# Three VectorE steps and one GpSimd step become two of each and a product: the exponentials that ScalarE does not take

## The chip, the cores and the metric

The kernel runs on one core of a Trainium2 chip. The metric is the device time of one execution in microseconds (us); three runs of the kernel before are given, and one further execution was recorded by the hardware profiler. The engines are TensorE (PE in the profile), VectorE (DVE), ScalarE (ACT), GpSimd (POOL) and SyncE (SP), which issues most transfers.

## The reference, cut to what matters

The kernel computes `g * a + (1 - g) * b` for one sequence of 2048 rows of 1024 values in bf16. `g` is a sigmoid of a row sum, `a` a diagonal state-space layer (a complex recurrence over 2048 steps between two large products), and `b` attention over all rows (no mask):

```
q, k, v = split(x @ wqkv)          # 32 heads of 32
scores  = q @ k.T * 32 ** -0.5
p       = softmax(scores)
b       = (p @ v) @ wo
```

The softmax needs 32 x 2048 x 2048 exponentials, 134 million. They are the largest single piece of elementwise work, and the change is in how a small part of them is computed.

## The kernel before, in words

**Attention.** The 32 heads are taken in 8 groups of 4 heads, the queries of a group in 8 blocks of 256, the keys of a block in 8 bursts of 256. That makes 512 bursts, numbered p = 0 to 511; `pg` is the number within a group, 0 to 63. In a burst TensorE computes the scores of 4 heads x 256 queries x 256 keys (line L1624, eight matmuls into two of three score buffers in PSUM), ScalarE takes their exponential in two instructions of 128x1024 (L1643), and TensorE later multiplies the result with the values (L1709). After the eight bursts of a block VectorE divides by the row sums (L1722, L1723) and a transposing transfer puts the result into place (L1729).

**The exponentials that VectorE takes.** In some bursts ScalarE's second instruction covers only 768 of the 1024 columns (L1640). The other 256 go to VectorE: L1633 reads them from PSUM, scales them and stores a fixed-point number in the tile `xi`, whose upper 16 bits are the integer part and lower 16 bits the fraction of a power of two. ScalarE's instruction of that burst waits for L1633, because both read the same score buffer. Two such bursts make a pair of 128x512, which `x_ops` finishes: a cubic polynomial of the fraction `lo`, put together with the integer part `hi` so that the bits of a bf16 number come out. Before the change these are three steps of VectorE in f32 (L1667, L1668, L1664, all `scalar_tensor_tensor`, which is an operation with a scalar and two tensors) and one of GpSimd (L1665), which rounds to the 16 bits. Line L1688 is the matmul that uses the result.

`X_PLAN` lists the pairs. Each entry is a burst number divisible by 4; within a block of eight bursts, a block with two entries takes bursts 0, 2 and 4, 6, and a block with one entry takes bursts 0 and 4 (`X_AT`).

**Dense work between the bursts.** TensorE fills each burst with four large matmuls of other work, through one PSUM bank: projections of the next group (`d_qk` L1426, `d_v` L1445), the state-space layer's input product (`d_u`, L1457) and output product (`d_c`, L1504), and at the end the output product with `wo` (`d_out`, L1535). When such a chain ends, VectorE empties the bank (L1433, L1451, L1461, L1517, L1547), and the next chain waits for that. VectorE also does the recurrence itself, called items: four products, two scans (L1362) and sums on SBUF tiles (L1353). GpSimd copies the last state of a scan (L1365) and carries it on (L1396).

**What sets the order.** Every engine's program is written out in a fixed order by `build`, which keeps a model of VectorE's clock (`dve_t`): for each burst it puts as many waiting VectorE steps into the queue as fit by their listed costs, the steps of `x_ops` preferred where no chain ends in the burst. A step of `x_ops` has a cost in the first place of its tuple; nothing at run time reorders a queue. Semaphores between the engines follow from the tiles that each step reads and writes.

**Weights.** The projection weights lie in the tile `wb`: those for K and V in two buffers by the parity of the group, those for Q in one. `ld_w` loads 256 KB; K and V of group g+2 are loaded at pg = 25 of group g, Q of group g+1 at pg = 28. The rows of `wo` are later loaded into parts of `wb` and of the tile `cT`. `C_LOADS` is the burst from which the transposed loads of the C matrices start (L1081). All these go through SP's queue, as do the stores and loads of the items' inputs (L1462, L1474).

Of the kernel before, what the change touches and what calls it, by code (L numbers as in the profile page):

```python
# [922 lines left out]
GROUPS = 8  # L923
# [9 lines left out]
C_LOADS = 28  # L933

X_AT = ((0, 2), (4, 6), (0, 4))
X_PLAN = (64, 72, 80, 88, 92, 96, 100, 104, 108, 112, 116, 120, 124, 128, 132, 136, 144, 152, 160, 168, 172, 176, 180, 184, 188, 192, 200, 208, 216, 224, 228, 232, 236, 240, 244, 248, 252, 256, 260, 264, 272, 280, 288, 296, 304, 312, 316, 320, 324, 328, 332, 336, 344, 352, 356, 360, 364, 368, 372, 376, 380, 384, 388, 392, 396, 400, 404, 408, 412, 416, 420, 424, 428, 432, 436, 440, 444, 448, 452, 456, 460, 464, 468, 472, 476, 480, 484, 488, 492, 496, 500, 504)
X_COLS = 256
F_TS, F_ST = 1.32, 1.24
I_MM = 0.61
X_LAST = 0.735  # L940
# [4 lines left out]
E3, E2, E1, E0 = 0.0780245226404788, 0.2260671649, 0.6958335355, 0.9999252185627155  # L945
X_K = 128.0 * E3 / 65536.0 ** 3
# [12 lines left out]
class FastPath:  # L959

    def __init__(self, nc, S, es, d, flag):
        self.nc, self.S, self.d, self.flag = nc, S, d, flag
        E = es.enter_context
        T = lambda name, shape, dt: E(nc.sbuf_tensor("f_" + name, shape, dt))
# [8 lines left out]
        wb = T("wb", [128, 8192], BF)  # L973
        self.wq = wb[:, 0:1024].rearrange("p (a n) -> p a n", a=8)
        self.wkv = wb[:, 1024:5120].rearrange("p (s q a n) -> p s q a n", s=2, q=2, a=8)
        self.bT = wb[:, 5120:8192].rearrange("p (s a n) -> p s a n", s=3, a=8)

        row = lambda o, n: wb[:, o:o + 1024 * n].rearrange("p (a n) -> p a n", a=n)
        self.wo3 = [row(1024, 2), row(5120, 3), row(3072, 1), self.cT[0][:, 0:1, :], self.cT[0][:, 1:2, :]]
        self.wo = [(self.wo3[0][:, a, :], "wo0") for a in range(2)] + [(self.wo3[4][:, 0, :], "wo4")] + [(self.wo3[1][:, a, :], "wo1") for a in range(3)]  # L980
        self.wo += [(self.wo3[3][:, 0, :], "wo3"), (self.wo3[2][:, 0, :], "wo2")]
# [3 lines left out]
        hp = T("hp", [128, 2, 8, 512], BF)  # L985
        self.hp = hp
        self.hpx = wb[:, 5120:8192].rearrange("p (k n) -> p k n", k=6)
# [5 lines left out]
        self.xp = T("xp", [128, 2 * X_COLS], BF)  # L993
        self.ut = T("ut", [128, 2, 512], F32)
# [70 lines left out]
    def w_of(self, g, part):  # L1065
        return (self.wkv[:, g % 2, part - 1], ("w", g % 2, part)) if part else (self.wq, ("w", 0, 0))
# [586 lines left out]
    def x_ops(self, b):  # L1653

        xi, xq, xp = self.xi[:, b % 2], self.xq, self.xp
        lo = xi.bitcast(mybir.dt.uint16)[:, 0::2]
        hi = xi.bitcast(mybir.dt.int16)[:, 1::2]
        bits = xp.bitcast(mybir.dt.int16)[:]
        w = 65536.0
        i2, p2 = [("xi", b % 2, 0), ("xi", b % 2, 1)], [("xp", 0), ("xp", 1)]  # L1660

        def last():
            assert self.x_out == len(self.x_done)
            self.dve(lambda e: e.scalar_tensor_tensor(xq[:], hi, 128.0 / X_K, xq[:], ALU.mult, ALU.add), i2 + ["xq"], ["xq"], "x_q")  # L1664
            self.pool(lambda e: e.tensor_scalar(bits, xq[:], X_K, 128.0 * (E0 + 126.0), ALU.mult, ALU.add), ["xq"], p2, "x_p")  # L1665
            self.x_done.add(b)
        return [(0.73, 0.0, lambda: self.dve(lambda e: e.scalar_tensor_tensor(xq[:], lo, E2 / E3 * w, lo, ALU.add, ALU.mult), i2, ["xq"], "x_q")),  # L1667
                (0.73, 0.0, lambda: self.dve(lambda e: e.scalar_tensor_tensor(xq[:], xq[:], E1 / E3 * w * w, lo, ALU.add, ALU.mult), ["xq"] + i2, ["xq"], "x_q")),  # L1668
                (X_LAST, 0.0, last)]

# [63 lines left out]
    def build(self):  # L1734
# [10 lines left out]
        for part in (1, 2):  # L1745
            self.ld_w(1, part)
# [12 lines left out]
        for g in range(1, GROUPS):  # L1759
            for c in range(4):  # L1760
                proj[g][8 + c].after = max(16 * c, 32)
        proj[0] = [self.d_qk(0, 0, 2), self.d_qk(0, 0, 3)]
        us, cs = [], []
# [15 lines left out]
        outs, k = [], 0  # L1779
# [3 lines left out]
        cur = None  # L1783
        first = FIRST
        wo1 = wo6 = last = False
# [4 lines left out]
        for p in range(first, NBURST):  # L1790
            g, pg = divmod(p, 64)
# [48 lines left out]
            if p == 386:  # L1840
                self.dma(lambda e: e.dma_start(self.wo3[0], wsv[:, 0:2, :]), [], ["wo0"] + [("w", 0, q) for q in (1, 2)], "ld_wo")
            if not cs and cur is None and not wo1 and self.c_left[3] == 0:
                wo1 = True
                self.dma(lambda e: e.dma_start(self.wo3[1], wsv[:, 3:6, :]), [], ["wo1"] + [("bT", r) for r in range(3)] + [("hp", 8, k) for k in range(6)], "ld_wo")
            if g >= 6 and not wo6 and not cs and self.c_left[3] == 0:
                wo6 = True
                self.dma(lambda e: e.dma_start(self.wo3[3], wsv[:, 6:7, :]), [], ["wo3", ("cT", 0, 0), ("cTf", 0, 0, 0), ("cTf", 0, 0, 1)], "ld_wo")
                self.dma(lambda e: e.dma_start(self.wo3[4], wsv[:, 2:3, :]), [], ["wo4", ("cT", 0, 1), ("cTf", 0, 1, 0), ("cTf", 0, 1, 1)], "ld_wo")
            if g >= 6 and not last and not proj[7] and not us and not cs and cur is None and not self.bg:

                last = True
                xs = [("xr", r) for r in range(16)]
                assert wo1 and wo6
                self.dma(lambda e: e.dma_start(self.wo3[2], wsv[:, 7:8, :]), [], ["wo2"] + [("w", 1, q) for q in (1, 2)] + xs, "ld_wo")
# [101 lines left out]
    def tail(self):  # L1956
# [41 lines left out]
        for r in range(2):  # L1998
            for cb in range(2):
                bank = 2 + r + 2 * cb  # L2000
                w = dict(acc=[("tb", bank)]) if cb == 0 else dict(writes=[("tb", bank)] + ([("S", 2)] if r == 0 else []), **({} if r == 0 else dict(acc=[("S", 2)])))
                S.op("pe", lambda e, r=r, cb=cb, bank=bank: e.matmul(ps[:, bank, :], OT[:, 7, 1792 + 128 * r:1920 + 128 * r], wo[7][0][:, 512 * cb:512 * (cb + 1)],
                                                                    start=(cb == 1), stop=True), reads=[("OT", 7, 7, r), "wo2"], name="tail", **w)
# [132 lines left out]
```

## Time and profile before

| | |
|---|---|
| median of 3 runs | 927.41 us (926.35 to 927.49) |
| profiled execution, its own time | 928.11 us |
| its span, first to last instruction | 926.3 us |
| granted TensorE clock, mean | 0.996 |
| ScalarE busy | 907.3 us, 98% |
| TensorE busy | 902.5 us, 97% |
| VectorE busy | 758.4 us, 82% |
| GpSimd busy | 86.8 us, 9% |
| pairs taken by VectorE | 92 |

The page gives each engine's busy time, the span in 40 slices with the busy share in tenths, the chain of work that ended last, and the costliest groups of instructions: line, engine, operation, output<-inputs, shapes, count, then busy time and mean duration, then the idle time before them and who ended it. The timeline gives the start, the length and the engine of single instructions, merged where they follow each other; idle time before an instruction stands in square brackets with its releaser. A mean of ScalarE's instructions is longer than their spacing, because one begins before the last has ended; spacing is read from starts.

### The profile page before, as it was taken

The page shows a single profiled execution, that of the slowest core. Times are in us where ns is not written, and L with a number is a line of the kernel's source. Part 1 is how long each engine was busy: PE and PEld are TensorE (multiplying, and loading weights), DVE is VectorE, ACT ScalarE, POOL GpSimd, SP SyncE. Part 2 cuts the span into 40 slices and gives each one's busy share as a digit, 9 for nine tenths or more (in the row PEclk, how much of TensorE's full clock was granted, in tenths as well). Part 3 has the DMA queues.
Part 4 walks back from the last instruction along what each step waited for, and adds up shares of the span by engine and source line. Part 5 has one row for each costly group of instructions (what it writes and reads, how often), then busy time and mean ns, then how long its engine had stood idle before and what let it go on. Part 6 is the DMA issues. An engine that isn't in the chain of part 4 may idle for free.

```text
span 926.3 us, 33979 instructions
## 1 busy us (share of the span) xinstructions
PE 902.5 (97%) x15316; PEld 503.9 (54%) x15316; DVE 758.4 (82%) x1310; ACT 907.3 (98%) x1034; POOL 86.8 (9%) x156
## 2 busy tenths in 40 slices
PE   8899999999999999999999999999999999999996
PEld 4554754557555565546655565555655655445553
DVE  2788989998989999989989999899988655776665
ACT  6999999999999999999999999999999999999996
POOL 2000000111000101011111020000010010001010
PEclk9999999999999999999999999999999999999998
DMA  9569747750457101272012511413001112424312
GB/s 195 87 116 184 93 84 138 144 116 5 81 113 152 50 20 49 67 147 53 19 51 65 126 45 31 104 63 103 20 15 43 31 51 77 156 83 128 114 62 75
DMA packets 170934, 77.69 MB, mean 84 GB/s; under 512 B 147232, under 2 KB 155424, under 8 KB 170784
## 3 DMA queue, kind: packets, MB, share of 16 engines
q1 hardware_dynamic: 168624, 74.94, 36.3%
q8 instruction: 121, 1.98, 0.9%
q10 hardware_dynamic: 2160, 0.53, 0.3%
q14 instruction: 29, 0.24, 0.1%
HBM read 25.18 MB, written 20.97 MB: 50 GB/s over the span
## 4 chain that ended last, share of the span: by engine, by line
PE 52%; ACT 40%; DVE 4%; DMA 2%; SPq 1%; issue 1%; POOL 0%; DVEq 0%; ACTq 0%
ACT f_pt L1643 32%; PE f_ps L1709 14%; PE f_ps L1624 10%; PE f_ps L1426 9%; PE f_ps L1504 7%; PE f_ps L1457 6%; ACT f_pt L1640 5%; PE f_ps L1445 5%; SPq L1062 1%; ACT f_cT L1643 1%; PE f_ps L1688 1%; DMA f_xT<-in_A_x_dram 1%; ACT f_Et L1643 1%; DMA f_wb<-in_A_B_im_dram 1%; DMA f_ub<-u_scratch 0%
## 5 line engine op out<-in xcount | busy, mean ns | idle before, releaser
L1643 ACT ACTIVATE f_pt<-f_ps 128x1024 bf16<-128x1024 f32 x760 | 728.8, 1090 | 1.5 <-PE f_ps L1624 1.3
L1709 PEld LDWEIGHTS f_ps<-f_V,f_pt 128*128 128x128 bf16 x7184 | 222.2, 96 | 95.3 <-issue 68.7
L1709 PE MATMUL f_ps<-f_V,f_pt 128*128 128x33 bf16 x7184 | 258.0, 178 | 0.0
L1624 PE MATMUL f_ps<-f_Q,f_K 32*128 32x256 bf16 x4096 | 203.3, 273 | 10.8 <-ACT f_pt L1643 3.3
L1640 ACT ACTIVATE f_pt<-f_ps 128x768 bf16<-128x768 f32 x184 | 165.3, 898 | 0.7 <-PE f_ps L1624 0.6
L1624 PEld LDWEIGHTS f_ps<-f_Q,f_K 32*128 32x128 bf16 x4096 | 60.7, 92 | 148.0 <-ACT f_pt L1643 120.6
L1457 PE MATMUL f_ps<-f_xT,f_wb 128*128 128x512 bf16 x512 | 131.5, 379 | 1.6 <-DMA f_wb<-in_A_B_im_dram 0.7
L1665 POOL TENSOR_SCALAR f_xp<-f_xq 128x512 int16<-128x512 f32 x92 | 67.3, 732 | 646.0 <-DVE f_xq L1664 471.3
L1426 PE MATMUL f_ps<-f_xT,f_wb 128*128 128x512 bf16 x464 | 119.3, 379 | 0.1
L1633 DVE TENSOR_SCALAR f_xi<-f_ps 128x256 int32<-128x256 f32 x184 | 77.4, 421 | 17.6 <-PE f_ps L1624 13.3
L1362 DVE TENSOR_TENSOR_SCAN f_ht<-f_pf,f_init,f_ut 128x512 bf16<-128x512 f32 x64 | 81.3, 1279 | 0.0
L1504 PE MATMUL f_ps<-f_cT,f_hp 128*128 128x512 bf16 x272 | 74.5, 379 | 0.1
L1667 DVE SCALAR_TENSOR_TENSOR f_xq<-f_xi 128x512 f32<-128x512 uint16 x92 | 63.7, 692 | 3.2
L1668 DVE SCALAR_TENSOR_TENSOR f_xq<-f_xq,f_xi 128x512 f32<-128x512 f32 x92 | 63.6, 692 | 3.1
L1664 DVE SCALAR_TENSOR_TENSOR f_xq<-f_xi,f_xq 128x512 f32<-128x512 int16 x92 | 63.5, 690 | 2.6
L1457 PEld LDWEIGHTS f_ps<-f_xT,f_wb 128*128 128x128 bf16 x512 | 40.1, 96 | 40.5 <-issue 8.6
L1535 PE MATMUL f_ps<-f_wb,f_OT 128*128 128x512 bf16 x188 | 61.2, 381 | 0.4 <-DVE f_Et L1547 0.4
L1445 PE MATMUL f_ps<-f_wb,f_xT 128*128 128x128 bf16 x896 | 59.3, 219 | 0.0
L1426 PEld LDWEIGHTS f_ps<-f_xT,f_wb 128*128 128x128 bf16 x464 | 36.1, 96 | 35.6 <-issue 7.6
L1461 DVE CAST f_ub<-f_ps 128x512 bf16<-128x512 f32 x64 | 44.1, 688 | 10.4 <-PE f_ps L1457 9.7
L1445 PEld LDWEIGHTS f_ps<-f_wb,f_xT 128*128 128x128 bf16 x896 | 50.4, 97 | 3.8 <-issue 3.8
L1722 DVE RECIPROCAL f_rc<-f_ps 128x8 f32<-128x8 f32 x63 | 13.1, 207 | 47.6 <-PE f_ps L1688 43.5
(149 smaller groups left out, 822.5 us busy)
## 6 DMA issues: line engine op xcount, KB each, us to landing
u_scratch<-f_ub SPq DMA_DIRECT2D x64, 128.0 KB, 2.1
f_ub<-u_scratch SPq DMA_DIRECT2D x32, 256.0 KB, 3.0
ag_scratch<-f_Ag SPq DMA_DIRECT2D x32, 256.0 KB, 2.0
f_hp<-ag_scratch SPq DMA_DIRECT2D x32, 256.0 KB, 3.0
f_wb<-in_B_wqkv_dram SPq DMA_DIRECT2D x21, 256.0 KB, 4.1
out_dram<-f_xT SPq DMA_DIRECT2D x16, 256.0 KB, 2.2
f_OT<-f_On SPq DMA_TRANSPOSE x63, 2.3
f_wb<-in_B_wo_dram SPq DMA_DIRECT2D x1, 768.0 KB
```

Source lines behind the costliest of these rows:

```text
L1362: ops.append((1.24, lambda ri=ri: dve(lambda e: e.tensor_tensor_scan(ht[:, ri, :], rr, ut[:, ri, :], self.init[:, ri, j:j + 1], ALU.mult, ...
L1426: mms.append((1, lambda e, f, l, a=a, w=w: e.matmul(ps[:, bank, :], w[:, a, :], xT[:, a, 512 * ch:512 * (ch + 1)], start=f, stop=l), [tok] ...
L1445: m = e.matmul(ps[:, bank, 128 * q:128 * (q + 1)], xT[:, a, 128 * kt:128 * (kt + 1)], w[:, a, :], start=(a == 0), stop=(a == 7))
L1457: mms.append((1, lambda e, f, l, a=a: e.matmul(ps[:, 7, :], bT[:, (2 * n + ri) % 3, a, :], xT[:, a, 512 * ch:512 * (ch + 1)], start=f, sto ...
L1504: mms.append((1, lambda e, f, l, j=j, ri=ri, h=h: e.matmul(ps[:, 7, :], h[:, cols], cT[ri][:, j, 512 * cb:512 * (cb + 1)], start=f, stop=l ...
L1624: m = e.matmul(ps[:, 2 * sl[h // 2] + h % 2, 256 * kl:256 * (kl + 1)], K[32 * h:32 * h + 32, g % 2, 128 * kt:128 * (kt + 1)], Q[32 * h:32 ...
L1633: first = self.dve(lambda e: e.tensor_scalar(self.xi[:, b % 2, X_COLS * n:X_COLS * (n + 1)], ps[:, 2 * s + 1, 512 - X_COLS:512], X_A, X_LO ...
L1640: self.S.op("act", lambda e: e.activation(flat(self.tile[p]), flat(ps[:, 2 * s:2 * s + 2, :]), ACT.Exp, scale=SCALE), reads=[("S", s)], wr ...
L1643: self.act(lambda e: e.activation(self.tile[p], ps[:, 2 * s:2 * s + 2, :], ACT.Exp, scale=SCALE), [("S", s)], [("pt", p)], "exp")
L1665: self.pool(lambda e: e.tensor_scalar(bits, xq[:], X_K, 128.0 * (E0 + 126.0), ALU.mult, ALU.add), ["xq"], p2, "x_p")
L1667: return [(0.73, 0.0, lambda: self.dve(lambda e: e.scalar_tensor_tensor(xq[:], lo, E2 / E3 * w, lo, ALU.add, ALU.mult), i2, ["xq"], "x_q") ...
L1709: m = e.matmul(ps[:, 6, o:o + 33], self.tile[p][:, h2, 256 * kl + 128 * qt:256 * kl + 128 * (qt + 1)], V[:, g % 2, 2 * i + kl, h, :], star ...
```

## The change: what it does

The cubic has one real root, -X_R, so it factors into (lo + X_R) times a quadratic. GpSimd now makes the linear factor first (`x_l`, 16-bit integers to f32, written to the new tile `xl`) and then the power of two (`x_e`, from `hi`, written as bf16 bits to the new tile `xe`). VectorE makes the quadratic's first part (`x_q`, as before), then the product of quadratic and linear factor (`x_m`, f32 in, bf16 out, new tile `xm`), and last the product of `xm` and `xe` in bf16 (`x_p`). The order of emission is: `x_l` on GpSimd, `x_q` on VectorE, `x_e` on GpSimd, `x_m`, `x_p`. The planned cost of the last step goes from 0.735 to 0.36.

Eight entries are added to `X_PLAN` (84, 204, 268, 276, 284, 292, 300, 308), so 100 pairs; in each case a block with one entry becomes a block with two. To make room for the new tiles `wb` shrinks from 8192 to 6144 columns: the weights of K and V have one buffer instead of two. Their loads move to pg = 0 of the group before (for group 1, V's at the start and K's at burst 17), Q's load to pg = 38, and the projections of K start no earlier than pg = 4, those of Q no earlier than pg = 42. The C loads start at burst 32 instead of 28. The rows of `wo` have new places, and seven of the eight are loaded together when the last output product of the state-space layer is done.

```diff
-C_LOADS = 28
+C_LOADS = 32
+W_AT = (38, 0, 17)
...
-X_LAST = 0.735
+X_LAST = 0.36
...
-X_K = 128.0 * E3 / 65536.0 ** 3
+X_R = 1.8383391859372556
+X_B, X_C = E2 / E3 - X_R, E0 / (E3 * X_R)
...
-        wb = T("wb", [128, 8192], BF)
+        wb = T("wb", [128, 6144], BF)
+        self.wqkv = [wb[:, 1024 * k:1024 * (k + 1)].rearrange("p (a n) -> p a n", a=8) for k in range(3)]
...
+        self.xl = T("xl", [128, 2 * X_COLS], F32)
+        self.xm = T("xm", [128, 2 * X_COLS], BF)
+        self.xe = T("xe", [128, 2 * X_COLS], BF)
...
     def w_of(self, g, part):
-        return (self.wkv[:, g % 2, part - 1], ("w", g % 2, part)) if part else (self.wq, ("w", 0, 0))
+        return self.wqkv[part], ("w", 0, part)
...
-        bits = xp.bitcast(mybir.dt.int16)[:]
+        bits = self.xe.bitcast(mybir.dt.int16)[:]
...
+        def start():
+            self.pool(lambda e: e.tensor_scalar(self.xl[:], lo, E3 / w ** 3, E3 * X_R / w ** 2, ALU.mult, ALU.add), i2, ["xl"], "x_l")
+            self.dve(lambda e: e.scalar_tensor_tensor(xq[:], lo, X_B * w, lo, ALU.add, ALU.mult), i2, ["xq"], "x_q")
+            self.pool(lambda e: e.tensor_scalar(bits, hi, 128.0, 128.0 * 127.0, ALU.mult, ALU.add), i2, ["xe"], "x_e")
+
         def last():
             assert self.x_out == len(self.x_done)
-            self.dve(lambda e: e.scalar_tensor_tensor(xq[:], hi, 128.0 / X_K, xq[:], ALU.mult, ALU.add), i2 + ["xq"], ["xq"], "x_q")
-            self.pool(lambda e: e.tensor_scalar(bits, xq[:], X_K, 128.0 * (E0 + 126.0), ALU.mult, ALU.add), ["xq"], p2, "x_p")
+            self.dve(lambda e: e.tensor_tensor(xp[:], self.xm[:], self.xe[:], ALU.mult), ["xm", "xe"], p2, "x_p")
             self.x_done.add(b)
-        return [(0.73, 0.0, lambda: self.dve(lambda e: e.scalar_tensor_tensor(xq[:], lo, E2 / E3 * w, lo, ALU.add, ALU.mult), i2, ["xq"], "x_q")),
-                (0.73, 0.0, lambda: self.dve(lambda e: e.scalar_tensor_tensor(xq[:], xq[:], E1 / E3 * w * w, lo, ALU.add, ALU.mult), ["xq"] + i2, ["xq"], "x_q")),
+        return [(0.73, 0.0, start),
+                (0.73, 0.0, lambda: self.dve(lambda e: e.scalar_tensor_tensor(self.xm[:], xq[:], X_C * w * w, self.xl[:], ALU.add, ALU.mult), ["xq", "xl"], ["xm"], "x_m")),
                 (X_LAST, 0.0, last)]
...
-        for part in (1, 2):
-            self.ld_w(1, part)
+        self.ld_w(1, 2)
...
-            if pg == 25 and g + 2 < GROUPS:
-                assert g or not (proj[0] or cur and cur.tag == "proj")
-                for part in (1, 2):
-                    self.ld_w(g + 2, part)
-            if pg == 28 and g + 1 < GROUPS:
-                assert not (cur and cur.tag == "proj")
+            if pg == W_AT[1 if g else 2] and g + 1 < GROUPS:
+                self.ld_w(g + 1, 1)
+                if g:
+                    self.ld_w(g + 1, 2)
+            if pg == W_AT[0] and g + 1 < GROUPS:
+                assert not proj[0]
                 self.ld_w(g + 1, 0)
```

More of the change, by code (lines that the diff above doesn't have):

```diff
@@ L1760, in build @@
             for c in range(4):
-                proj[g][8 + c].after = max(16 * c, 32)
+                proj[g][c].after = W_AT[1] + 4
+                proj[g][8 + c].after = max(16 * c, W_AT[0] + 4)
         proj[0] = [self.d_qk(0, 0, 2), self.d_qk(0, 0, 3)]
@@ L1784, in build @@
         first = FIRST
-        wo1 = wo6 = last = False
+        wo1 = last = False
         nal = nc = 0
@@ L1838, in build @@
+            if pg == W_AT[0] and g + 1 < GROUPS:
+                assert not proj[0]
                 self.ld_w(g + 1, 0)
             wsv = self.d["B_wo"].rearrange("(a p) n -> p a n", p=128)
-            if p == 386:
-                self.dma(lambda e: e.dma_start(self.wo3[0], wsv[:, 0:2, :]), [], ["wo0"] + [("w", 0, q) for q in (1, 2)], "ld_wo")
-            if not cs and cur is None and not wo1 and self.c_left[3] == 0:
+            if not wo1 and not cs and cur is None and self.c_left[3] == 0:
@@ L1843, in build @@
                 wo1 = True
[L1844 to L1848, printed above, removed]
+                for a in range(7):
+                    j = a if a < 3 else a - 3
+                    x = [("cT", 0, j), ("cTf", 0, j, 0), ("cTf", 0, j, 1)]
+                    if a in (3, 4, 5):
+                        x = [("bT", a - 3)] + [("hp", 8, k) for k in (2 * a - 6, 2 * a - 5)]
+                    self.dma(lambda e, a=a: e.dma_start(self.wo[a][0], wsv[:, a, :]), [], ["wo%d" % a] + x, "ld_wo")
@@ L1849, in build @@
             if g >= 6 and not last and not proj[7] and not us and not cs and cur is None and not self.bg:
                 last = True
-                xs = [("xr", r) for r in range(16)]
-                assert wo1 and wo6
-                self.dma(lambda e: e.dma_start(self.wo3[2], wsv[:, 7:8, :]), [], ["wo2"] + [("w", 1, q) for q in (1, 2)] + xs, "ld_wo")
+                assert wo1
+                self.dma(lambda e: e.dma_start(self.wo[7][0], wsv[:, 7, :]), [], ["wo7", ("cT", 0, 4), ("cTf", 0, 4, 0), ("cTf", 0, 4, 1)], "ld_wo")
```

16 lines of the change are left out of this document (7 added, 9 removed).

## Prediction

> **What bounds the kernel now.** I read the page's first two parts, the groups, and then the same busy times by stage.
>
> ```profile
> span 926.3 us, 33979 instructions
> PE 902.5 (97%) x15316; PEld 503.9 (54%) x15316; DVE 758.4 (82%) x1310; ACT 907.3 (98%) x1034; POOL 86.8 (9%) x156
> ...
> DVE  2788989998989999989989999899988655776665
> ACT  6999999999999999999999999999999999999996
> ```
>
> ```profile
> 140.00:700.00 560.00, 556.11 (x9501) 311.60 (x9501) 506.19 (x816) 559.22 (x638) 62.20 (x100) 1.00 0.33 74
> 700.00:926.30 226.30, 215.59 (x3617) 116.30 (x3615) 148.93 (x304) 218.18 (x253) 18.53 (x31) 0.98 0.27 82
> ...
> 500.00:540.00 40.00, 39.58 (x656) 21.01 (x649) 37.51 (x60) 40.00 (x46) 5.27 (x6) 1.00 0.44 106
> ```
>
> The columns after the stretch's length are TensorE, its weight loads, VectorE, ScalarE and GpSimd. ScalarE is busy in 559.2 of the 560 us between 140 and 700: its exponentials bound that stage. VectorE is at 506.2 of 560, 90%, and its fullest row of 40 us is 37.5, 94%, with ScalarE still at 40.0. After 700 it has room: 148.9 of 226.3. So columns moved off ScalarE shorten the kernel as long as VectorE keeps up, and in the long middle stage it has about 50 us in hand, part of it waits that it can't use.
>
> **What a pair is worth to ScalarE.** Its own timeline, where the plan passes from one pair per eight bursts to two:
>
> ```profile
> 547.50 0.98 ACT L1640 ACTIVATE f_pt<-f_ps 128x768 bf16<-128x768 f32 x1
> ...
> 554.62 0.98 ACT L1640 ACTIVATE f_pt<-f_ps 128x768 bf16<-128x768 f32 x1
> ...
> 572.37 0.93 ACT L1640 ACTIVATE f_pt<-f_ps 128x768 bf16<-128x768 f32 x1
> 573.11 2.93 ACT L1643 ACTIVATE f_pt<-f_ps 128x1024 bf16<-128x1024 f32 x3
> 575.84 0.91 ACT L1640 ACTIVATE f_pt<-f_ps 128x768 bf16<-128x768 f32 x1
> 576.55 2.95 ACT L1643 ACTIVATE f_pt<-f_ps 128x1024 bf16<-128x1024 f32 x3
> 579.27 0.93 ACT L1640 ACTIVATE f_pt<-f_ps 128x768 bf16<-128x768 f32 x1
> ```
>
> With one pair, four bursts take 554.62 - 547.50 = 7.12 us, eight 14.24. With two pairs two bursts take 3.47 and 3.43, eight 13.80. The eight blocks that get a second pair give 8 x 0.44 = 3.5 us, if nothing else stops ScalarE.
>
> **The pair on VectorE, before.**
>
> ```profile
> 571.51 0.41 DVE L1633 TENSOR_SCALAR f_xi<-f_ps 128x256 int32<-128x256 f32 x1
> 571.96 0.69 DVE L1667 SCALAR_TENSOR_TENSOR f_xq<-f_xi 128x512 f32<-128x512 uint16 x1
> 572.68 0.69 DVE L1668 SCALAR_TENSOR_TENSOR f_xq<-f_xq,f_xi 128x512 f32<-128x512 f32 x1
> 573.41 0.69 DVE L1664 SCALAR_TENSOR_TENSOR f_xq<-f_xi,f_xq 128x512 f32<-128x512 int16 x1
> 574.07 0.69 DVE L1433 CAST f_Q<-f_ps 128x512 bf16<-128x512 f32 x1
> ...
> 574.19 0.62 POOL L1665 TENSOR_SCALAR f_xp<-f_xq 128x512 int16<-128x512 f32 x1 [7.64 <-DVE f_xq L1664]
> ```
>
> L1633's second half of the pair ends at 571.92; the three steps follow back to back and end at 574.10, 2.18 us later. The dense bank's cast starts at once behind them. GpSimd's step, 0.62 us, starts 0.09 after the third step and runs beside the cast, which reads PSUM.
>
> **The pair after, if the two engines didn't disturb each other.** The first step is the old one (0.69), `x_m` has its shape (0.69), and `x_p`, a product of 512 bf16 columns, is like the 0.42 of this row:
>
> ```profile
> L1353 DVE TENSOR_TENSOR f_hp<-f_ut,f_tq 128x512 bf16<-128x512 bf16 x17 | 7.1, 417 | 0.0
> ```
>
> GpSimd's `x_l` would start 0.09 after L1633 and end at 0.71, so `x_m` starts about 0.77, after the 0.73 of `x_q`; `x_e` is done by 1.3, before `x_m` at 1.5. The chain ends about 1.9 after L1633: 0.28 less than before.
>
> **But they share something.** These rows, VectorE's and GpSimd's, are what the forecast turns on:
>
> ```profile
> 267.97 1.28 DVE L1320 SCALAR_TENSOR_TENSOR f_cT<-f_cT,f_pf,f_OT 128x1024 bf16<-128x1024 bf16 x1
> ...
> 268.13 1.59 POOL L1665 TENSOR_SCALAR f_xp<-f_xq 128x512 int16<-128x512 f32 x1 [10.90 <-DVE f_xq L1664]
> ...
> 550.62 1.28 DVE L1362 TENSOR_TENSOR_SCAN f_ht<-f_pf,f_init,f_ut 128x512 bf16<-128x512 f32 x1
> 551.93 0.91 DVE L1353 TENSOR_TENSOR f_tq<-f_ht,f_Et 128x1024 bf16<-128x1024 bf16 x1
> ...
> 550.79 1.52 POOL L1665 TENSOR_SCALAR f_xp<-f_xq 128x512 int16<-128x512 f32 x1 [12.13 <-DVE f_xq L1664]
> ...
> L1353 DVE TENSOR_TENSOR f_ut<-f_ht,f_Et 128x1024 bf16<-128x1024 bf16 x32 | 21.9, 685 | 0.0
> ```
>
> The same GpSimd step takes 0.62 beside a cast from PSUM and 1.52 to 1.59 beside a VectorE operation that reads two SBUF tensors. It ends a fixed time after that operation: 268.13 + 1.59 = 269.72, 0.47 after 269.25; 552.31, 0.41 after 551.90. It is held until VectorE's operation is over. The other way round, the product that starts at 551.93 under a running GpSimd step takes 0.91 instead of 0.685 and ends 0.53 after that step. One of the two waits for the other.
>
> Before the change GpSimd's step mostly falls beside a cast. Now both of its steps are released by L1633, at the moment when VectorE starts `x_q`, and all of `x_q`, `x_m`, `x_p` read two SBUF tensors. VectorE is first: in the rows above it starts 0.04 after L1633, GpSimd 0.09 after its releaser. So, counted from the end of L1633:
> - `x_q` 0.04 to 0.73; `x_l` is held and ends 0.41 to 0.48 later, at 1.14 to 1.21. `x_m` waits for it.
> - `x_e` is next in GpSimd's queue, already released, and runs another 0.57 to 0.62, to about 1.75; `x_m`, started beside it, is held and ends 0.53 later, at 2.28.
> - `x_p` 0.42 and a gap of 0.03: 2.73.
> If `x_m` gets in ahead of `x_e`, it ends at 1.93, `x_e` at 2.4, `x_p` at 2.86. So the chain is 0.55 (to 0.68) us longer than before, not 0.28 shorter; the plan, which reserves 0.73 + 0.73 + 0.36 = 1.82, fills the difference with other steps and is 0.9 short per pair. I take +0.55, since it follows from the row with a product behind GpSimd; the ends for the range are -0.28 and +0.68.
>
> The Trainium skill states the rule behind these rows ("SBUF — State Buffer", section "Who interferes with whom"): a VectorE instruction with two SBUF inputs contends with a GpSimd instruction that reads SBUF, and the second to issue fully blocks until the first is done. The trace agrees that one blocks, but of GpSimd's 0.62 us only 0.41 to 0.48 come after the release, so a part of it is not blocked. By full blocking, 0.73 + 0.62 + 0.62 + 0.69 + 0.45, the chain would be 3.1 us, and the sum below would come out 70 x 0.38 / 0.98 = 27 us higher. The rows have durations for it, so they are used.
>
> **What that costs.** How many pairs fall into each stage:
>
> ```profile
> 140.00:700.00 560.00, 42.72 (x62) 1.00 0.33 74
> 700.00:926.30 226.30, 20.77 (x30) 0.98 0.27 82
> ```
>
> Middle stage: 506.2 + 62 x 0.55 (34) + 8 new pairs x (2 x 0.42 for L1633 + 2.73) (29) = 569, less some 4 us by which the old GpSimd step held products (an estimate: the 64 of the row below are each 0.027 longer than 0.685, 1.7 us, and the other products are held likewise), so 565 us of VectorE's time in a stage that is 560 long and that ScalarE alone would shorten to 556.5.
>
> ```profile
> L1353 DVE TENSOR_TENSOR f_ut<-f_ht,f_tq 128x512 f32<-128x512 bf16 x64 | 43.4, 712 | 0.7
> ...
> DVE f_rc L1722 <- PE f_ps L1688: 43.5, 50, 1.8
> ```
>
> VectorE becomes the bound, and its queue is in order: L1633 (on which ScalarE waits) and the casts of the single dense bank (on which TensorE waits, and behind TensorE's wait the next scores) stand behind the chain. At 100% busy the stage is 565 long (+5), at the 94% of the fullest row 601 (+41). VectorE's largest idle time is its wait for a block's last matmul, 43.5 us in all in 50 waits; that shrinks when VectorE is the late one, so I take 98%: 576, +16.
>
> Late stage: 30 pairs, VectorE at 66%. What stands behind the chain there:
>
> ```profile
> 867.49 0.75 DVE L1547 SCALAR_TENSOR_TENSOR f_xT<-f_ps,f_gcol,f_hp 128x512 bf16<-128x512 f32 x1
> ...
> 868.47 0.59 PE L1535 MATMUL f_ps<-f_wb,f_OT 128*128 128x512 bf16 x2
> 869.49 0.12 PEld L1624 LDWEIGHTS f_ps<-f_Q,f_K 32*128 32x128 bf16 x8 [0.49 <-ACT f_pt L1643]
> ```
>
> The bank is read out by 868.24, the next chain starts 0.23 later, and TensorE then waits 0.49 for ScalarE. A delay of 0.55 becomes one of 0.3 on TensorE, which that wait covers: 0, at most 30 x 0.2 = 6. I take +1.
>
> **Transfers.** The opening has one stall that the moves touch:
>
> ```profile
> 68.14 1.28 SPq L1071 DMA_DIRECT2D f_wb<-in_B_wqkv_dram  x1
> 69.53 0.67 SPq L1474 DMA_DIRECT2D f_ub<-u_scratch  x1
> ...
> 73.34 0.69 DVE L1353 TENSOR_TENSOR f_ht<-f_ub,f_Et 128x1024 bf16<-128x1024 bf16 x1 [2.39 <-DMA f_ub<-u_scratch]
> ...
> 77.36 1.94 ACT L1643 ACTIVATE f_OT<-f_ps 128x1024 bf16<-128x1024 f32 x2 [1.34 <-PE f_ps L1624]
> ...
> f_wb<-in_B_wqkv_dram SPq DMA_DIRECT2D x21, 256.0 KB, 4.1
> ```
>
> At burst 28 the C loads and Q's weights stand in SP's queue ahead of an item's input; VectorE waits 2.39 for it and ScalarE loses 1.34. Both move to later bursts, where they can meet another item load: -1.34 to +1.34. The K and V loads move ahead of pg = 0 work in SP's queue (transposes of the block's result, item stores): the same kind of collision, at most once per group, and K's projection has four bursts, 7.1 us, against a landing time of 4.1, so 3 us to spare. The `wo` rows land together some 10 us before they are used. GpSimd's queue also carries L1365, which comes 0.6 later; the carry has a whole chunk's time. I take -1 for all of it, between -2 and +7.
>
> **Sum.** The profiled execution took 928.11 us, 0.7 above the median. 928.1 + 16 + 1 - 1 = 944.1; less 0.7, 943. The 3.5 us of ScalarE are inside the stage's 576.
>
> **Rivals.**
> 1. *The engines don't hold each other here* (faster). `x_q` reads 16-bit columns with a step, and no row shows GpSimd beside such a step; or the plan puts casts between the steps, as it does in part of the pairs. Then VectorE needs 506 - 4 - 62 x 0.28 + 8 x 2.74 = 507 in 556.5, 91%, and ScalarE stays the bound: 927.4 - 3.5 - 1 = 923. It decides at a chain that is no longer than before: at +0 VectorE would be at 506 - 4 + 8 x 3.02 = 526 of 556.5, the 94.5% that the fullest row shows without loss. Against it: L1320 is the same operation and holds GpSimd.
> 2. *Held, but VectorE's idle time takes it up*: 100% busy, +5 in the stage, nothing elsewhere, so 931; and with a chain of only +0.4, no change to speak of.
> 3. *Collisions of weight loads*: 7 groups x 1 us, on top of rival 1, 930. SP's queue rows above speak for one such case in the whole trace.
>
> **How the numbers follow.** 0.2% of 927.4, 1.9 us, is about what a measurement can tell from no change. VectorE held and the bound: 0.62, its own range 930 to 965 (100% to 95% busy, -2 to +7 for transfers). Rival 1: 0.26, 921 to 925. Rival 2: 0.08, half of it within 0.2%. Rival 3: 0.04. Faster 0.26, same 0.04, slower 0.70. The range of 8 in 10 takes rival 1 nearly whole and leaves out the slowest of the first case: 922 to 960.
>
> **What would show it.** Right: `x_l` (tensor `xl`) with a mean near 1.1 rather than 0.62, an idle time of about 0.4 before `x_m` put down to GpSimd, `x_m` near 1.1 rather than 0.69, VectorE at 96% or more between 140 and 700, and ScalarE there below its 99.9%, waiting for scores or L1633. Wrong: `x_l` and `x_e` at 0.62 and `x_m` at 0.69 (rival 1), or these lengthened while ScalarE stays full (rival 2). The transfers are right if the gap at 77 is gone and no like gap stands at a group's start.

## The result and the profile after

The changed kernel takes 982.32 us (981.40 to 984.20, six runs) against 926.88 us (926.05 to 928.04) of the kernel before beside it: a ratio of 1.060, 95% interval 1.0586 to 1.0614. I had forecast 943, with 960 as the upper end. The sign was right, the size was 39 us short.

First the page of the changed kernel: span, busy times, and the slices of VectorE and ScalarE.

```profile
span 979.9 us, 34236 instructions
...
PE 910.2 (93%) x15316; PEld 509.5 (52%) x15316; DVE 780.1 (80%) x1350; ACT 919.6 (94%) x1034; POOL 194.0 (20%) x264
...
DVE  2789988888888889888899888888888655666665
ACT  6999999999999999999999999999999999999996
```

The span is 979.9 - 926.3 = 53.6 us longer. No engine got full by it: VectorE has gone from 82% to 80%, ScalarE from 98% to 94%. Something waits on something else in a ring. The place is found by comparing the starts of ScalarE's exponentials at the same bursts:

| bursts | before, us | after, us | difference |
|---|---|---|---|
| start to 64 | 131.0 | 128.9 | -2.1 |
| 64 to 392 (middle) | 576.2 | 620.2 | +44.0 |
| 392 to the end (late) | 219.1 | 230.8 | +11.7 |

The busy times by stretch of the changed kernel, columns as in the prediction (length, TensorE, its weight loads, VectorE, ScalarE, GpSimd); the last row is the middle stage by bursts:

```profile
140.00:700.00 560.00, 521.83 (x8786) 291.42 (x8787) 488.90 (x795) 527.29 (x593) 123.64 (x164) 1.00 0.31 70
...
129.00:749.20 620.20, 578.20 (x9765) 323.87 (x9762) 539.17 (x878) 584.10 (x658) 137.53 (x180) 1.00 0.30 70
```

The same bursts of the kernel before:

```profile
131.00:707.20 576.20, 572.26 (x9765) 319.80 (x9762) 520.74 (x838) 575.42 (x657) 62.40 (x101) 1.00 0.33 75
```

ScalarE was busy for 575.4 of 576.2 us; now for 584.1 of 620.2. It is no longer the bound. The steps of a pair, from the groups of the changed kernel:

```profile
L1667 POOL TENSOR_SCALAR f_xl<-f_xi 128x512 f32<-128x512 uint16 x100 | 111.9, 1119 | 581.2 <-DVE f_xi L1637 581.2
...
L1676 DVE SCALAR_TENSOR_TENSOR f_xm<-f_xq,f_xl 128x512 bf16<-128x512 f32 x100 | 112.2, 1122 | 58.2 <-POOL f_xl L1667 58.2
...
L1668 DVE SCALAR_TENSOR_TENSOR f_xq<-f_xi 128x512 f32<-128x512 uint16 x100 | 69.2, 692 | 3.4
...
L1669 POOL TENSOR_SCALAR f_xe<-f_xi 128x512 int16<-128x512 int16 x100 | 62.1, 621 | 7.9
...
L1673 DVE TENSOR_TENSOR f_xp<-f_xm,f_xe 128x512 bf16<-128x512 bf16 x100 | 42.3, 423 | 11.1 <-PE f_ps L1696 8.8
```

These are the signs that the prediction had named: `x_l` at 1.12 instead of 0.62, an idle time of 0.58 before each `x_m` put down to GpSimd, `x_m` at 1.12 instead of 0.69. One pair on the timeline of the changed kernel:

```profile
584.75 0.41 DVE L1637 TENSOR_SCALAR f_xi<-f_ps 128x256 int32<-128x256 f32 x1
...
585.20 0.69 DVE L1668 SCALAR_TENSOR_TENSOR f_xq<-f_xi 128x512 f32<-128x512 uint16 x1
585.25 1.12 POOL L1667 TENSOR_SCALAR f_xl<-f_xi 128x512 f32<-128x512 uint16 x1 [6.46 <-DVE f_xi L1637]
...
586.45 0.62 POOL L1669 TENSOR_SCALAR f_xe<-f_xi 128x512 int16<-128x512 int16 x1
586.48 1.13 DVE L1676 SCALAR_TENSOR_TENSOR f_xm<-f_xq,f_xl 128x512 bf16<-128x512 f32 x1 [0.58 <-POOL f_xl L1667]
...
587.53 0.68 DVE L1357 TENSOR_TENSOR f_ut<-f_ht,f_tq 128x512 f32<-128x512 bf16 x1
...
588.13 0.68 DVE L1455 CAST f_V<-f_ps 128x512 bf16<-128x512 f32 x1
588.73 0.40 DVE L1637 TENSOR_SCALAR f_xi<-f_ps 128x256 int32<-128x256 f32 x1
...
588.96 0.59 PE L1430 MATMUL f_ps<-f_xT,f_wb 128*128 128x512 bf16 x2 [0.46 <-DVE f_V L1455]
```

`x_l` ends at 586.37, 0.48 after `x_q`. GpSimd then starts `x_e` 0.08 later and VectorE starts `x_m` 0.11 later, so `x_e` is always first in, and `x_m` ends at 587.61, 0.54 after `x_e`. The dense bank's cast stands behind these steps and a product of the recurrence, and TensorE waits 0.46 for it. The rest of the ring, from the waits of the middle stage (columns: us in total, times, longest):

```profile
DVE f_xm L1676 <- POOL f_xl L1667: 41.3, 70, 0.9
...
ACT f_pt L1647 <- PE f_ps L1628: 18.7, 56, 0.7
...
ACT f_pt L1644 <- DVE f_xi L1637: 16.4, 38, 0.8
DVE f_rc L1730 <- PE f_ps L1696: 13.1, 27, 1.2
PE f_ps L1461 <- DVE f_ub L1465: 11.1, 19, 1.1
...
DVE f_xp L1673 <- PE f_ps L1696: 5.7, 17, 0.4
```

ScalarE's two waits, 18.7 and 16.4, are nearly all of the 36 us in which it is idle. TensorE's listed waits for read-outs by VectorE, of which the line with L1461 is the largest, add up to some 40 us in this window, against 0.2 before. In the same bursts of the kernel before, ScalarE's whole wait for scores was

```profile
ACT f_pt L1643 <- PE f_ps L1624: 0.7, 3, 0.3
```

So VectorE stands still for `x_l`, TensorE waits for VectorE's casts, ScalarE waits for TensorE's scores and for L1637, and VectorE waits again for TensorE. And in the late stage of the changed kernel:

```profile
917.15 1.13 DVE L1676 SCALAR_TENSOR_TENSOR f_xm<-f_xq,f_xl 128x512 bf16<-128x512 f32 x1 [0.58 <-POOL f_xl L1667]
...
918.32 0.42 DVE L1673 TENSOR_TENSOR f_xp<-f_xm,f_xe 128x512 bf16<-128x512 bf16 x1
...
918.66 0.74 DVE L1551 SCALAR_TENSOR_TENSOR f_xT<-f_ps,f_gcol,f_hp 128x512 bf16<-128x512 f32 x1
...
919.47 0.82 PE L1539 MATMUL f_ps<-f_cT,f_OT 128*128 128x512 bf16 x3 [0.40 <-DVE f_xT L1551]
...
920.89 2.86 ACT L1647 ACTIVATE f_pt<-f_ps 128x1024 bf16<-128x1024 f32 x3 [0.29 <-PE f_ps L1628]
```

TensorE waits 0.40 for the bank, and ScalarE behind it 0.29 for scores. A block of eight bursts in this stage (from burst 464 on; "late blocks" below) takes 14.88 us here and 13.81 before.

### The profile page after: what moved, and what is told of

Read it like the earlier page. It is cut to its first block, busy times and chain, and to the rows that moved or that the text cites. A ratio compares the mean times of both kernels' runs of the same rounds, so it can differ in the third digit from the quotient of the medians.

```text
span 979.9 us, 34236 instructions
## 1 busy us (share of the span) xinstructions
PE 910.2 (93%) x15316; PEld 509.5 (52%) x15316; DVE 780.1 (80%) x1350; ACT 919.6 (94%) x1034; POOL 194.0 (20%) x264
## 4 chain that ended last, share of the span: by engine, by line
PE 60%; DVE 24%; POOL 6%; ACT 4%; issue 4%; SPq 1%; DMA 1%; DVEq 0%
PE f_ps L1717 13%; PE f_ps L1628 10%; PE f_ps L1508 9%; PE f_ps L1461 9%; PE f_ps L1430 8%; POOL f_xl L1667 6%; DVE f_xm L1676 5%; PE f_ps L1539 5%; PE f_ps L1449 4%; DVE f_ub L1465 2%; DVE f_xp L1673 2%; DVE f_xi L1637 2%; ACT f_pt L1647 2%; DVE f_ut L1357 2%; DVE f_Ag L1521 1%
## 5 line engine op out<-in xcount | busy, mean ns | idle before, releaser
L1647 ACT ACTIVATE f_pt<-f_ps 128x1024 bf16<-128x1024 f32 x744 | 707.5, 1046 | 26.1 <-PE f_ps L1628 25.4
L1667 POOL TENSOR_SCALAR f_xl<-f_xi 128x512 f32<-128x512 uint16 x100 | 111.9, 1119 | 581.2 <-DVE f_xi L1637 581.2
L1676 DVE SCALAR_TENSOR_TENSOR f_xm<-f_xq,f_xl 128x512 bf16<-128x512 f32 x100 | 112.2, 1122 | 58.2 <-POOL f_xl L1667 58.2
L1461 PE MATMUL f_ps<-f_xT,f_wb 128*128 128x512 bf16 x512 | 131.5, 379 | 13.5 <-DVE f_ub L1465 11.1
L1637 DVE TENSOR_SCALAR f_xi<-f_ps 128x256 int32<-128x256 f32 x200 | 83.2, 416 | 4.1 <-PE f_ps L1628 2.9
L1668 DVE SCALAR_TENSOR_TENSOR f_xq<-f_xi 128x512 f32<-128x512 uint16 x100 | 69.2, 692 | 3.4
L1461 PEld LDWEIGHTS f_ps<-f_xT,f_wb 128*128 128x128 bf16 x512 | 40.2, 96 | 53.9 <-issue 22.0
L1669 POOL TENSOR_SCALAR f_xe<-f_xi 128x512 int16<-128x512 int16 x100 | 62.1, 621 | 7.9
L1539 PE MATMUL f_ps<-f_cT,f_OT 128*128 128x512 bf16 x156 | 45.2, 381 | 8.6 <-DVE f_xT L1551 6.3
L1673 DVE TENSOR_TENSOR f_xp<-f_xm,f_xe 128x512 bf16<-128x512 bf16 x100 | 42.3, 423 | 11.1 <-PE f_ps L1696 8.8
```

What stands on the lines that cost most here:

```text
L1461: mms.append((1, lambda e, f, l, a=a: e.matmul(ps[:, 7, :], bT[:, (2 * n + ri) % 3, a, :], xT[:, a, 512 * ch:512 * (ch + 1)], start=f, sto ...
L1539: mms.append((1, lambda e, f, l, j=j: e.matmul(ps[:, 7, :], OT[:, j, 256 * qb + 128 * r:256 * qb + 128 * (r + 1)], wo[j][0][:, 512 * cb:51 ...
L1637: first = self.dve(lambda e: e.tensor_scalar(self.xi[:, b % 2, X_COLS * n:X_COLS * (n + 1)], ps[:, 2 * s + 1, 512 - X_COLS:512], X_A, X_LO ...
L1647: self.act(lambda e: e.activation(self.tile[p], ps[:, 2 * s:2 * s + 2, :], ACT.Exp, scale=SCALE), [("S", s)], [("pt", p)], "exp")
L1667: self.pool(lambda e: e.tensor_scalar(self.xl[:], lo, E3 / w ** 3, E3 * X_R / w ** 2, ALU.mult, ALU.add), i2, ["xl"], "x_l")
```

## The experiments

The theory: the two engines exclude each other where both read SBUF, and VectorE's fixed order passes the wait on. The rivals: the longer list of pairs, the new plan, the moved transfers, or a wait that I had not seen. "Chain" below is the time from the end of a pair's second L1637 to the end of its last VectorE step; in the kernel before it is 2.18, in the changed one 2.90. All ratios are against the kernel before on the same chip, with 95% intervals; its median there was between 928.3 and 930.3 us.

**GpSimd writes only.** The linear factor and the power of two are left out; constants of the same shape are written in their place.

```diff
-self.pool(lambda e: e.tensor_scalar(self.xl[:], lo, E3 / w ** 3, E3 * X_R / w ** 2, ALU.mult, ALU.add), i2, ["xl"], "x_l")
+self.pool(lambda e: e.memset(self.xl[:], E3 * (0.5 + X_R) / w ** 2), i2, ["xl"], "x_l")
-self.pool(lambda e: e.tensor_scalar(bits, hi, 128.0, 128.0 * 127.0, ALU.mult, ALU.add), i2, ["xe"], "x_e")
+self.pool(lambda e: e.memset(self.xe[:], 1.0), i2, ["xe"], "x_e")
```

> GpSimd's two steps write constants of the right size and read nothing; all else, the plan and the order included, is the changed kernel's. The exponentials of the 100 pairs are therefore not computed. Theory (GpSimd's reads of SBUF and VectorE's steps with two SBUF inputs hold each other): x_m starts at 0.77 after L1637 and lasts 0.69, the chain ends at 1.9, and the time is 921 to 926 us. Rival A (the moved and single-buffered weight loads cost the time): 975 to 985, as the changed kernel. Rival B (VectorE has too much to do with 100 pairs, whoever holds whom): 950 or more. If writes are held too, x_l stays near 1.1 us and the time near 982.

Measured 947.73 us (946.75 to 947.98), 1.0196 (1.0174 to 1.0217). The hold is gone, but the time is not what either theory gave. From its groups and then its waits:

```profile
L1667 POOL MEMSET f_xl<- 128x512 f32 x100 | 52.5, 525 | 625.3 <-DVE f_xi L1637 625.3
...
L1676 DVE SCALAR_TENSOR_TENSOR f_xm<-f_xq,f_xl 128x512 bf16<-128x512 f32 x100 | 69.2, 692 | 3.9 <-POOL f_xe L1669 0.3
```

```profile
DVE f_xp L1673 <- PE f_ps L1696: 42.0, 36, 1.6
```

`x_m` is at 0.69 again, beside GpSimd steps that write; two thirds of the loss are gone. What is left is a wait that I had missed: `x_p` writes the single tile `xp`, which TensorE may still be reading for the pair before (L1696). Before the change GpSimd wrote `xp`, and the wait stood in GpSimd's queue, with little behind it. Now it stands in VectorE's queue, with the casts and L1637 behind it.

**The old steps in the new frame.** The changed kernel with its 100 pairs, its plan and its moved transfers, but the four old steps; and the kernel before with the moved transfers alone, 92 pairs.

```diff
-X_PLAN = (64, 72, 80, 84, 88, 92, ...
+X_PLAN = (64, 72, 80, 88, 92, ...      # the second kernel only
...
-X_LAST = 0.36
+X_LAST = 0.735                         # the second kernel only
...
-        return [(0.73, 0.0, start), ...
+        return [(0.73, 0.0, lambda: self.dve(lambda e: e.scalar_tensor_tensor(xq[:], lo, E2 / E3 * w, lo, ALU.add, ALU.mult), i2, ["xq"], "x_q")), ...
```

> The changed kernel with the four old steps in place of the new ones, and the same plan (its last step still planned at 0.36, though it takes 0.72), the same 100 pairs and transfers. Theory: the chain is back at 2.18 us, GpSimd works beside a cast again, VectorE's time in the middle stage is about 506 + 8 x 3.02 = 530 of 557 us: 927 to 940 us. Rival A: 970 or more. Rival B: 965 or more, since VectorE's own instructions are more than in the changed kernel.

Measured 930.73 us (929.51 to 931.66), 1.0005 (0.9991 to 1.0019): eight more pairs, the short planned cost and the new loads cost nothing together against the kernel before.

> The kernel before with the transfers of the changed one: single weight buffers, the new load times, C loads from burst 32, the new places of wo. Old steps, old costs, 92 pairs. Theory: the gap of 1.34 us on ScalarE at 77 us is gone and nothing as large comes: 924.5 to 927 us. Rival A: 960 or more. Rival B: 927.

Measured 926.22 us (925.70 to 928.91), 0.9968 (0.9956 to 0.9980): the moved transfers are a gain of 0.3%, the only part of the change that is one. This kernel beats both. Against it the eight pairs and the short planned cost, with the old steps, are 4.5 us.

**The changed steps with the old list of 92 pairs.**

```diff
-X_PLAN = (64, 72, 80, 84, 88, 92, ...
+X_PLAN = (64, 72, 80, 88, 92, ...
```

> The changed kernel with the 92 old entries of X_PLAN. Theory: every pair loses by the held chain, the eight new ones only a little more than they save: 972 to 982 us. Rival A: 982 to 986. Rival B (the eight pairs overfill VectorE): 927 to 940.

Measured 974.46 us (973.87 to 975.08), 1.0489 (1.0467 to 1.0511). The eight pairs are worth some 8 to 10 us of the loss (982.3 - 974.5, or 1.060 - 1.049 of 928); 48 us, against the run with the moves alone, belong to the steps themselves and the place that they write to.

**A place of its own for `x_p`.** The product goes into the first half of the pair's own `xi`, which is double and read out by then; so nothing waits for the pair before. Once with the writes only, once with the real steps.

```diff
+    def x_to(self, b):
+        return self.xi[:, b % 2, 0:X_COLS].bitcast(BF)
...
-        xi, xq, xp = self.xi[:, b % 2], self.xq, self.xp
+        xi, xq, xp = self.xi[:, b % 2], self.xq, self.x_to(b)
...
```

> As the run in which GpSimd only writes constants, and x_p writes its product into the pair's own half of xi, which has two buffers, instead of into the single tile xp. Theory: what was left there, 20 us, is x_p waiting on VectorE's queue for the last pair's matmul (L1696), 42 us in 36 waits; without that wait 921 to 927 us, and the blocks after burst 464 at 13.81. Rival: the new plan with its 100 pairs is too full by itself: 938 to 948.

Measured 923.67 us (923.00 to 925.04), 0.9941 (0.9922 to 0.9959). The wait is gone, the chain is 1.9, late blocks are at 13.81. That is the 923 of rival 1: what the change would be worth if the engines did not hold each other.

> The changed kernel with x_p written into the pair's own half of xi, so that it never waits for the last pair's matmul; GpSimd computes both steps. Theory: the chain is still 2.90 us after L1637, of the 55 us only the 8.8 us of waits before x_p go, the blocks after burst 464 stay at 14.88: 970 to 980 us. Rival (that wait is the main cost): 945 or less.

Measured 973.78 us (972.91 to 975.27), 1.0489 (1.0458 to 1.0520). Against 982.3 the wait for L1696 was 8.5 (8.3 by the spans of the two profiled executions); late blocks go from 14.88 to 14.56. The other 50 us above 923.7 come from two GpSimd steps that read. (A step that writes takes 0.525 where one that reads takes 0.62 alone; that 0.1 is small beside an `x_l` of 1.12.)

**Only one of the two reads.** From the last kernel, `x_l` (first run) or `x_e` (second run) written as a constant; that factor is left out.

> x_p in the pair's own half of xi; x_l only writes a constant (the linear factor is left out), x_e reads. Theory: x_l is done by 0.6, x_e is held by x_q and ends near 1.2, x_m is held by x_e and ends near 1.75, the chain near 2.2 us as in the kernel before: 922 to 932 us, late blocks 13.8. If each held step cost the same by itself: 950.

Measured 932.12 us (931.87 to 933.17), 1.0030 (1.0013 to 1.0047). `x_m` is held to 1.06 but waits for nothing; the chain is 2.28, 0.10 longer than before the change, and late blocks are at 13.81. The time is a tenth above the range.

> x_p in the pair's own half of xi; x_e only writes a constant (the power of two is left out), x_l reads. Theory: x_l is held to 1.2, x_m runs 1.3 to 2.0, the chain ends near 2.46 us: between the two, 930 to 955 us, late blocks 13.9 to 14.3.

Measured 939.65 us (939.25 to 940.05), 1.0118 (1.0082 to 1.0154). `x_m` is at 0.69 with 57.9 us of waits for `x_l`; the chain is 2.46. Late blocks stay between 13.78 and 13.89, where 13.9 to 14.3 had been expected: a chain 0.28 longer than before costs the late stage next to nothing. The four kernels in a row, by spans of the stages:

| what reads | chain, us | bursts 64 to 392 | 392 to the end | time |
|---|---|---|---|---|
| neither | 1.91 | 573.2 | 219.1 | 923.67 |
| `x_e` | 2.28 | 581.6 | 219.0 | 932.12 |
| `x_l` | 2.46 | 588.8 | 220.0 | 939.65 |
| both | 2.90 | 615.3 | 227.2 | 973.78 |

Both together cost the middle stage 42.1, more than 8.4 + 15.6: the loss grows faster than the chain.

**The C loads alone.** Which of the moves gains?

```diff
-C_LOADS = 28
+C_LOADS = 32
```

> The kernel before with one line changed: the C loads start at burst 32 instead of 28. The run with all the moved transfers gained 0.3% (926.2 against 930.0) without any of the new arithmetic. If that gain is the opening stall at burst 28, where the C loads stand in SP's queue ahead of an item's input: the gap of 1.34 us on ScalarE there goes, the four bursts around it give up to 2 us, ratio 0.997 to 0.9985. If it is the weight loads of K, V and Q that gained: ratio 1.000 (0.999 to 1.001), and the gap stays because Q's load at burst 28 is still there.

Measured 927.35 us (925.68 to 929.64), 0.9975 (0.9958 to 0.9992). The interval overlaps that of all moves, and ScalarE's gap of 1.34 at 77 us is gone from the timeline. This one line makes up most, perhaps all, of the gain; the weight loads gain nothing that shows.

**The bank read out first, late stage only.** In the kernel with a place of its own, from burst 448 on `x_m` and `x_p` are kept back until the dense bank has been emptied.

```diff
+            self.x_hold = self.p >= 448                  # when x_q is emitted
...
+                    if self.x_hold and len(self.xbg) % 3:
+                        break                            # x_m, x_p not yet
...
-                    if c == X_LAST:
+                    if c == X_LAST or self.p >= 448 and len(self.xbg) % 3 == 0:
...
                 ended.evac()
+                self.x_hold = False
```

> The changed kernel with x_p in the pair's own half of xi, and from burst 448 on VectorE empties the dense bank before x_m and x_p instead of after them; the two engines still exclude each other as before. If the late stage loses time because TensorE waits for a bank that stands behind the chain: its blocks of eight bursts fall from 14.56 to 13.8 us, eight blocks, so 6 us less than 973.8: 966 to 969. If it loses time because the pairs take VectorE or the score buffers too long whatever stands where (the chain still lasts 2.9): blocks stay at 14.4 to 14.6, and the time at 972 to 975. If the pair now comes too late for its own matmul, blocks get longer than 14.6.

Measured 968.24 us (967.66 to 969.45), 1.0416 (1.0393 to 1.0439). Late blocks are at 13.81 again. Its timeline there:

```profile
905.67 0.69 DVE L1672 SCALAR_TENSOR_TENSOR f_xq<-f_xi 128x512 f32<-128x512 uint16 x1
905.72 1.12 POOL L1671 TENSOR_SCALAR f_xl<-f_xi 128x512 f32<-128x512 uint16 x1 [5.33 <-DVE f_xi L1637]
...
906.92 0.62 POOL L1673 TENSOR_SCALAR f_xe<-f_xi 128x512 int16<-128x512 int16 x1
...
907.74 0.75 DVE L1551 SCALAR_TENSOR_TENSOR f_xT<-f_ps,f_gcol,f_hp 128x512 bf16<-128x512 f32 x1 [1.37 <-PE f_ps L1539]
...
908.81 0.68 DVE L1680 SCALAR_TENSOR_TENSOR f_xm<-f_xq,f_xl 128x512 bf16<-128x512 f32 x1
```

The GpSimd steps are as long as ever, but VectorE stands at the bank when TensorE ends it, and `x_m` finds both results ready.

**Kept apart everywhere.** The same from burst 64 on with 92 pairs, and from burst 208 on with 100 pairs (where `x_m` stays right behind `x_q` in 28 pairs).

```diff
-            self.x_hold = self.p >= 448
+            self.x_hold = self.p >= 64      # 208 in the second kernel
...
```

> The changed kernel with x_p in the pair's own half of xi, the old list of 92 pairs, and in every pair the step x_m kept back until after the next read-out of the dense bank, so that VectorE never stands at x_m while x_l runs. The engines still exclude each other: two GpSimd steps of 0.62 per pair. If the loss is VectorE standing still for x_l (0.58) and x_m held by x_e (0.43), both of which follow from x_m standing right behind x_q: x_m back to 0.69 with an idle time near 0, x_l still 1.1; a pair then costs VectorE 1.8 of its own plus at most 0.43 by which x_e holds a neighbour, 2.2 to 2.3 in the worst case, where the run with x_l written only had 932: 924 to 936. If the exclusion itself is the loss, so that the time only moves to other VectorE operations that are held or hold x_l longer: 955 to 972.

Measured 936.51 us (935.53 to 937.43), 1.0088 (1.0063 to 1.0113), half a microsecond above the range. Its groups:

```profile
L1671 POOL TENSOR_SCALAR f_xl<-f_xi 128x512 f32<-128x512 uint16 x92 | 101.9, 1108 | 524.1 <-DVE f_xi L1637 501.6
...
L1680 DVE SCALAR_TENSOR_TENSOR f_xm<-f_xq,f_xl 128x512 bf16<-128x512 f32 x92 | 62.6, 680 | 0.0
...
L1673 POOL TENSOR_SCALAR f_xe<-f_xi 128x512 int16<-128x512 int16 x92 | 88.5, 962 | 7.3
L1366 DVE TENSOR_TENSOR_SCAN f_ht<-f_pf,f_init,f_ut 128x512 bf16<-128x512 f32 x64 | 88.5, 1399 | 0.0
```

and the scan in the page of the kernel before:

```profile
L1362 DVE TENSOR_TENSOR_SCAN f_ht<-f_pf,f_init,f_ut 128x512 bf16<-128x512 f32 x64 | 81.3, 1279 | 0.0
```

Against 974.46 with the same pairs, 38 us are gone: some 8 of them by the place for `x_p`, if it is worth with 92 pairs what it was with 100, and some 30 by the order alone. The exclusion is still there: `x_e` went from 0.62 to 0.96 and the scans from 1.28 to 1.40, and the stage from burst 64 to 392 takes 585.6 instead of 576.2. So with 92 pairs most of the loss was VectorE standing at `x_m` at the wrong moment, and a smaller part, some 10 us against the run with the moves alone, is the exclusion itself, moved to other operations.

> The same with the 100 pairs, kept apart from burst 208 on (28 of the pairs stand as in the changed kernel, all in the first 200 bursts). If standing still for x_l is the loss: the blocks from burst 208 on back to 13.8 to 14.1, the earlier two-pair blocks at 14.5 to 15.5 as before, so the loss of some 14 us up to burst 208 stays and the rest goes: 934 to 946. If the exclusion itself is: 960 to 973.

Measured 956.23 us (955.92 to 957.35), 1.0301 (1.0276 to 1.0326), between the two ranges. From burst 392 on it is at the times of the kernel before (219.4 us), but the bursts from 208 to 392 take 336.7 against 323.5 before and 346.6 in the kernel with a place of its own; the blocks that begin at 264, 272 and 280, three of those with a new pair, take 15.5 to 17.2 us. In these three blocks TensorE waits for `x_p` (L1677) before the pair's own matmul:

```profile
PE f_ps L1700 <- DVE f_xi L1677: 4.4, 3, 1.6
```

Kept back, the product comes too late. These three blocks take 48.5 us, against 43.4 in the kernel with a place of its own and 42.7 before. So here this order is worth less, 17.5 us of 50: 28 pairs stand as they did, and it brings a delay of its own.

## Why the prediction failed

**The hold was right.** Each step of "They share something" is in the trace: `x_q` free, `x_l` ending 0.48 after it, `x_e` first in, `x_m` held by it, 0.53 to 0.54. The chain came out at 2.90 where I had 2.73, so +0.72 per pair instead of +0.55: `x_l` ended at the upper end of my span for it, GpSimd's next step starts 0.08 after `x_l` where I had none, and it then takes its whole 0.62. The rule of the Trainium skill ("SBUF — State Buffer", "Summary: rules for kernel authors") that the second to issue fully blocks would, by the prediction's estimate, have made the chain 3.1; the traces show a held step ending 0.48 to 0.54 after the other, of 0.62 to 0.69 that it takes alone, so a part is not blocked. The Trainium skill also says ("SBUF — State Buffer", "Who interferes with whom") that a GpSimd instruction that only writes does not contend with two SBUF inputs; the runs with constants agree, `x_m` at 0.692 beside them.

**The 98% was the step that failed.** VectorE's work in the middle stage was nearly as I had it. Busy time, the wait for `x_l` and that for L1696 come to 539.2 + 41.3 + 5.7 = 586.2 us from burst 64 to 392. The kernel before has 520.7 in these bursts and 506.2 in the 560 us that I summed, 14.5 fewer; so 586.2 - 14.5 = 571.7 stands against my 565. But I divided by 98%, on the argument that VectorE's wait for a block's last matmul would shrink when VectorE is the late one. The stage ran at 586.2 / 620.2 = 94.5%, the share of the fullest row that I had quoted, and set aside with its +41. Of the miss of 28 us, 565 against 571.7 makes up 7 (at 98%); the other 21 are the share. The wait for a block's last matmul shrank, from 20.4 us to 13.1, but did not vanish. In all, VectorE's idle time outside the pair's own steps fell only from 55.5 us (576.2 - 520.7) to 34.0 (620.2 - 586.2), where 98% leaves some 12: what is left beside the 13.1 is its other waits for TensorE and gaps between instructions. The sign that I had named, VectorE 96% busy, did not come: it was busy for 87% and at 94.5% with its waits for the pair's own steps. The prediction priced the chain as VectorE's time alone; the runs show that it also matters what stands behind the chain. VectorE, late with a read-out, makes TensorE late (the 40 us above), and then waits for TensorE itself. That this gives 94.5% and not another share is read off here, not derived; with `x_e` alone held the same stage lost 8.4 us, against the kernel in which neither reads, at 92.7% busy.

**The late stage was the second.** I had worked out that TensorE would be 0.3 late per pair, and let a wait of 0.49 cover it. That row is one of the weight loader (PEld), not of the matmuls. TensorE's matmuls around it, in the kernel before:

```profile
869.11 0.38 PE L1535 MATMUL f_ps<-f_wb,f_OT 128*128 128x512 bf16 x1
...
869.49 0.40 PE L1624 MATMUL f_ps<-f_Q,f_K 32*128 32x256 bf16 x8
```

and at the same place in the changed kernel:

```profile
920.13 0.38 PE L1539 MATMUL f_ps<-f_wb,f_OT 128*128 128x512 bf16 x1
...
920.44 0.12 PEld L1628 LDWEIGHTS f_ps<-f_Q,f_K 32*128 32x128 bf16 x8 [0.42 <-issue]
920.44 0.40 PE L1628 MATMUL f_ps<-f_Q,f_K 32*128 32x256 bf16 x8
```

In the second the loader's row is idle for 0.42 although it waits for nothing that the profile shows, and the matmuls start 0.31 apart, in the first 0.38. So of the 0.49 only 0.07 was time that TensorE had over. The 0.3 was too small as well: TensorE waits 0.40 in the row shown, and from burst 448 on a block of two pairs loses 1.07, 0.53 per pair. The blocks from 392 to 448 lose less (3.7 us for 14 pairs); in all it is +11.7 instead of +1, and 3.6 of it went with the wait for L1696. The kernel with the bank read out first shows the mechanism: the GpSimd steps as long as ever, the blocks back at 13.81.

**A wait was missed.** I did not ask who else uses the tile that `x_p` writes when its step moves to VectorE. It costs 8.5 us in the changed kernel and 24 with constants.

**The transfers** were forecast at -1 and gave -2.1 up to burst 64, -1.3 in the kernel with the moves alone; no stall at a group's start took their place.

**The rivals.** Rival 1 needed the engines not to hold each other; made so, the kernel takes 923.67, its number, but only with the place for `x_p` changed too; without that it is 947.73. Rival 2, held but taken up by idle time, did not happen. With `x_e` alone the time is near its 931 (932.12), but by luck: the chain there is only 0.10 longer than before, and VectorE is busy for 92.7% of the middle stage, not 100%. Rival 3's collisions of weight loads did not appear.

## What to carry to other kernels

Moving a step to another engine is two questions beyond its duration: does it read SBUF beside an operation with two SBUF inputs, and does the engine that waits for its result stand still, with work behind it in its queue that other engines need? Put something between the request and the use; here that order was worth some 30 us with 92 pairs, with not one instruction fewer, and 17.5 in the kernel with 100, where 28 pairs stood as before and in three blocks the product came too late. When a queue becomes the bound, give a reason for any share above the fullest that the profile shows; here the fullest row, 94%, was nearer than my 98%. Read TensorE's slack from the starts of its matmuls, not from the idle time of the weight loader. And for every step that changes engine look up who still reads what it writes.

## What was not expected of the hardware

- A held step is not simply queued behind the other: an `x_m` that is 0.69 alone ends 0.53 to 0.54 after GpSimd's step, an `x_l` that is 0.62 alone 0.48 after VectorE's, in every one of the 100 pairs.
- The scan is held too, and holds: in the kernel kept apart with 92 pairs, a scan that takes 1.28 alone took 1.63 beside `x_l`, and the `x_e` behind it 1.40 instead of 0.62.
- When `x_l` ends, GpSimd's own next instruction gets in ahead of the VectorE step that waited for `x_l`, in all 100 pairs: `x_e` starts 0.08 after it, `x_m` 0.10 or more.
